# Half-chunk attention from chunk 8 on, and k and v by head through the weights' buffers, in a fused retention and FFN kernel

## The chip, the core and the metric

The kernel runs on one core of a Trainium2 chip. The metric is the device time of one execution in microseconds (us). The engines are named as in the profile: PE is TensorE's matmul, PEld its weight load, DVE is VectorE, ACT is ScalarE, POOL is GpSimd, SP is SyncE, which here issues every DMA.

## What is computed

A recurrent retention layer (batch 4, 8 heads, 768 tokens, head dimension 64) whose output goes through a feed-forward layer with squared ReLU (512 to 2048 to 512), all inputs and the output in float32:

```
for t in range(S):
    state = gamma * state + outer(k[:, :, t], v[:, :, t])      # per batch and head
    y[:, :, t] = scale * q[:, :, t] @ state
x = y as [3072 tokens, 512]
out = relu(x @ w_in) ** 2 @ w_out
```

## The kernel before, in words

**Chunks.** The 3072 tokens are 24 chunks of 128, six to a batch; chunk m is number i = m mod 6 of its batch. Inside a chunk the recurrence is done as matrix products: scores of k against q, a mask, scores times v, plus q times the state that the chunks before have left (`s_bd`). The factors of gamma are multiplied into q and k (`scale_q`, `scale_kv`, `scale_k2`). Heads go in four pairs; "block-diagonal" buffers (`k_bd`, `v_bd`, `s_bd`, `ks_bdp`) hold one head of the pair on partitions 0 to 63 and the other on 64 to 127, with zeros beside them, so that one 128-row matmul serves both heads.

**Three ways of doing a chunk.** Chunks 0 to 3 are done as two pairs ahead of everything else. Chunks 4 to 11 take whole chunks (`attend`): 8 score matmuls of 128 columns (L421) in two steps with a mask each (L428, DVE), 4 state matmuls of 128 columns (L447) and 4 + 8 output matmuls of 128 columns (L476, L484); the PSUM state `c_ps` then also holds products across the two heads of a pair, which nobody reads. Chunks 12 to 23 take two halves of 64 tokens (`attend2`): 8 score matmuls of 64 columns (L681) with one mask (L688), 2 x 4 state matmuls of 64 columns (L708) into a compact `c_ps`, and 8 + 8 output matmuls of 64 columns (L730, L737). q is transposed by PE up to chunk 7 and by DMA from chunk 8 on; k likewise, and for chunks 8 to 11 DVE spreads the DMA's result into `k_bd` (`spread_k`, L410).

**The FFN** runs in blocks of 4, 2, 2, ... chunks. Its matmuls (L777 for the first product, L835 for the second) fill PE; they are cut into pieces of 0.86 to 0.89 us. Pieces are numbered on from 5: block 0 has 12 of the first product (places 5 to 16) and 16 of the second (17 to 32); block 1 is 33 to 40 and 41 to 48, block 2 is 49 to 56 and 57 to 64, and so on by 16.

**The order is written by hand.** `put(n, step, m)` queues a step of the attention, a load or a cast behind piece n; `before(n)` emits the steps of place n in the order of their `put`, and the squares of h after them. Each engine runs its own instructions strictly in that order, waiting on semaphores; so a step that waits holds all that stands behind it on its engine. That holds for SP too: a DMA that waits for its input or its buffer holds every later load and store.

**Loads.** Weights come into `wstage`, 5 buffers of 1 MB, in the order w_in 0 to 3, w_out 0 to 3, and are cast to bf16. k and v of chunks 4 to 11 come a chunk at a time into `ldpool` (L113); those of chunks 12 to 23 in groups of three chunks, head by head, into `grpool` (L129, 16 DMAs of 96 KB a group). `pack_constants` and the zeros of the half-chunk buffers (`zero_off_diagonal`, L329) are made at places 50 to 64.

Of the kernel before, what the change touches and what calls it, by code (L numbers as in the profile page):

```python
# [9 lines left out]
FP32 = mybir.dt.float32  # L10
# [4 lines left out]
ALU = mybir.AluOpType  # L15
# [4 lines left out]
LDBUFS = 4  # L20

# [12 lines left out]
def kernel(  # L34
# [32 lines left out]
    ldpool = ctx.enter_context(tc.tile_pool(name="ldpool", bufs=LDBUFS // 2))  # L67
    grpool = ctx.enter_context(tc.tile_pool(name="grpool", bufs=2))
    qspool = ctx.enter_context(tc.tile_pool(name="qspool", bufs=2))
    kspool = ctx.enter_context(tc.tile_pool(name="kspool", bufs=4))  # L70
# [6 lines left out]
    wstage = ctx.enter_context(tc.tile_pool(name="wstage", bufs=5))  # L77
# [43 lines left out]
    def group_loads(m):  # L121

        b, i = chunks[m]
        for name, src, to in (("kg", k, raw_k), ("vg", v, raw_v)):
            t = grpool.tile([P, 2 * GROUP, NPAIR, D], FP32, name=name)
            for h in range(H):
                p, hh = divmod(h, 2)
                rows = slice(64 * hh, 64 * (hh + 1))
                nc.sync.dma_start(  # L129
                    t[rows, :, p, :],  # L130
                    src[b, h, i * C : (i + GROUP) * C, :].rearrange("(w s) d -> s w d", s=64),
                )
                yield
            for j in range(GROUP):
                to[m + j] = t[:, 2 * j : 2 * j + 2].rearrange("s u p d -> s (u p) d")

    w_in_v = moe_w_in.rearrange("(cb p) f -> p cb f", p=P)
# [3 lines left out]
    def load_w_in(g, parts=1):  # L141
        t = wstage.tile([P, NCB, FQ], FP32, name="w_stage")
        n = FQ // parts
        for j in range(parts):
            nc.sync.dma_start(
                t[:, :, j * n : (j + 1) * n], w_in_v[:, :, g * FQ + j * n : g * FQ + (j + 1) * n]
            )
        staged["in", g] = t

    def load_w_out(g):  # L150
        t = wstage.tile([P, FPQ, DM], FP32, name="w_stage")
        nc.sync.dma_start(t[:], w_out_v[:, g * FPQ : (g + 1) * FPQ, :])
        staged["out", g] = t
# [16 lines left out]
    halves = [slice(0, 64), slice(64, 128)]  # L170
# [160 lines left out]
    def scale_q(m):  # L331
        b, i = chunks[m]
        qs = qspool.tile([P, 2, H, D], BF16, name="qs")
        nc.vector.tensor_tensor(  # L334
            out=qs[:],
            in0=raw_q.pop(m).rearrange("s h r d -> s r h d"),
            in1=qf[:, i : i + 2, :, None].to_broadcast([P, 2, H, D]),
            op=ALU.mult,
        )
        at[m]["qs"] = qs  # L340

    def scale_kv(m):
        b, i = chunks[m]
        ks = kspool.tile([P, H, D], BF16, name="ks")
        nc.vector.tensor_tensor(
            out=ks[:],
            in0=raw_k.pop(m)[:],
            in1=kf[:, i, :, None].to_broadcast([P, H, D]),
            op=ALU.mult,
        )  # L350
# [47 lines left out]
    def dma_transpose_k(m):  # L398
        a = at[m]
        kT = kTpool.tile([P, 2 * NPAIR, C], BF16, name="kT")  # L400
        nc.sync.dma_start_transpose(kT[:, 0:NPAIR], a["ks"].rearrange("s h d -> s (h d)"))
        a["kT"] = kT

    def spread_k(m):
        a = at[m]
        kT = a.pop("kT")
        k_bd = k_bds[m % 2]
        for hh in range(2):
            rows = slice(64 * hh, 64 * (hh + 1))
            nc.vector.tensor_copy(k_bd[rows, :, hh, :], kT[rows, 0:NPAIR])  # L410
        a["k_bd"] = k_bd

# [24 lines left out]
    def state(m, on_scalar=1):  # L437

        b, i = chunks[m]
        a = at[m]  # L440
        if i == NCH - 1:
            return
        if i == 0:
            c_ps[0] = ps_c.tile([P, NPAIR, 2, D], FP32, name="c_ps")
        c = c_ps[0]
        for p in range(NPAIR):
            nc.tensor.matmul(  # L447
                c[:, p],
                lhsT=a["ks"][:, 2 * p : 2 * p + 2, :],
                rhs=a["v_bd"][:, p, ::3, :],  # L450
                start=(i == 0 and p == 0),
                stop=True,
                skip_group_check=True,
            )
        s_bd = s_bds[m % 2]
        for hh in range(2):
            rows = slice(64 * hh, 64 * (hh + 1))
# [11 lines left out]
    def outputs(m):  # L469
# [4 lines left out]
        for p in range(NPAIR):  # L474
            if i > 0:
                nc.tensor.matmul(  # L476
                    y[:, p, :],
                    lhsT=s_bds[(m - 1) % 2][:, p],
                    rhs=a["qT"][:, :, p, :],
                    start=True,  # L480
                    stop=False,
                )
            for hh in range(2):
                nc.tensor.matmul(  # L484
                    y[:, p, :],
                    lhsT=a["v_bd"][:, p, 2 * hh : 2 * hh + 2, :],
                    rhs=a["pt"][:, p, hh, :],
                    start=(i == 0 and hh == 0),
                    stop=(hh == 1),
                )  # L490
# [12 lines left out]
    def scale_pair_q(m, r, engine=nc.vector):  # L503
        b, i = chunks[m]
        if r == 0:
            at[m]["qs"] = qspool.tile([P, 2, H, D], BF16, name="qs")
        engine.tensor_tensor(
            out=at[m]["qs"][:, r],
            in0=raw_q[m].rearrange("s h r d -> s r h d")[:, r],
            in1=qf[:, i + r, :, None].to_broadcast([P, H, D]),  # L510
            op=ALU.mult,
        )

    def scale_pair_k(m, r):
        b, i = chunks[m]
        at[m]["ks"] = pair_view(ks_bd2s[m // 2])
        nc.vector.tensor_tensor(
            out=at[m]["ks"][:, r],
            in0=raw_k[m][:, r],
            in1=kfp[:, i + r, :, None].to_broadcast([P, H, D]),  # L520
            op=ALU.mult,
        )
# [115 lines left out]
    def scale_k2(m):  # L638
# [232 lines left out]
    scale_pair_q(0, 0)  # L871
    scale_pair_q(0, 1)
# [8 lines left out]
    scale_pair_q(2, 0, nc.gpsimd)  # L881
    scale_pair_q(2, 1, nc.gpsimd)
# [50 lines left out]
    def attend_q(m, scaled, transposed):  # L933
        if m % 2 == 0:
            put(scaled, scale_q, m)
            put(transposed, dma_transpose_q if m >= DMA_FROM else transpose_q, m)

# [15 lines left out]
    def attend2(m, d):  # L953
        attend_q(m, d - 17, d - 15)
        put(d - 15, scale_k2, m)
        put(d - 15, cast_v2, m)
        put(d - 13, transpose_k2, m)
        put(d - 6, state2, m, 0)
# [26 lines left out]
    for m, d in zip(range(8, NCHUNK), done):
        if m < PACK_FROM:
            attend(m, d - 15 if d < 70 else d - 16, (d - 13, d - 7, d - 5, d - 3, d))
        else:
            attend2(m, d)
        if m + 3 < PACK_FROM:  # L990
            put(d - 13, load, m + 3)
        elif m + 3 < NCHUNK and (m + 3) % 2 == 0:
            put(d - 13, load_q, m + 3)
    for m, place in zip(range(PACK_FROM, NCHUNK, GROUP), (43, 67, 92, 116)):
        loads = group_loads(m)
        for j in range(2 * H):
            put(place + 3 * j // 2, next, loads)
        put(place + 3 * H, next, loads, None)
# [43 lines left out]
```

## Time and profile before

| what | us |
|---|---|
| runs shown | 215.21, 242.04, 214.72 (median 215.21) |
| the profiled execution | 214.73 |
| its span, first to last instruction | 212.9 |
| PE busy in the span | 204.5 (96%) |
| DVE, ACT, POOL busy | 129.4, 116.2, 50.6 |
| w_in_bf casts (L291), first start | 15.5 |
| w_out_bf casts by POOL (L301), first start | 29.2 |
| first half-chunk matmul (L708) | 101.5 |

Durations below are of the profiled execution. "Mean ns of one" of a matmul holds the way through the array; what a matmul takes from PE is the distance of its start to the next one's start, which the chain of waits shows as the share of a run of matmuls.

### The profile page before, as it was taken

Reading aid. Unit: us, or ns where it says so; the run is one execution under the profiler, and the core shown is the slowest. Engines: PE = TensorE matmul, PEld = TensorE weight load, DVE = VectorE, ACT = ScalarE, POOL = GpSimd, SP = SyncE. Lnnn points to the kernel's source line nnn. Section 1 sums busy time; section 2 is a strip of 40 time slices with the busy share of each in tenths; the row PEclk is TensorE's granted clock in tenths of the full one; section 3 lists DMA queues with packets and bytes.
Section 4 is the critical chain, followed back from the end, with each engine's and each line's share of the span. In section 5 each row is a group of like instructions: output and inputs, shape, how many; then the busy total and the mean of one; then the engine's idle time right before and its main releaser. Section 6 shows DMA issues by size and latency. Waiting matters only on the chain.

```text
span 212.9 us, 5128 instructions
## 1 busy us (share of the span) xinstructions
PE 204.5 (96%) x2077; PEld 142.1 (67%) x2077; DVE 129.4 (61%) x257; ACT 116.2 (55%) x216; POOL 50.6 (24%) x106
## 2 busy tenths in 40 slices
PE   5789999999999999999999999999999999999994
PEld 1467644558966975875875875875965965965853
DVE  4777875265585696796495595593694693640410
ACT  8365885358853643652663663652753754643631
POOL 5332466221110411025121323008122223000000
PEclk9889999999999999999999999999999999999999
DMA  6999999999969898599698698998795452401102
GB/s 162 290 317 383 386 386 258 293 242 274 276 172 201 199 197 145 161 207 182 164 197 191 154 189 188 152 194 202 164 240 127 99 80 72 102 0 49 52 0 99
DMA packets 90551, 39.65 MB, mean 186 GB/s; under 512 B 66336, under 2 KB 84000, under 8 KB 90528
## 3 DMA queue, kind: packets, MB, share of 16 engines
q1 hardware_dynamic: 90528, 39.33, 79.4%
q8 instruction: 16, 0.26, 0.6%
q14 instruction: 7, 0.06, 0.1%
HBM read 27.26 MB, written 6.29 MB: 158 GB/s over the span
## 4 chain that ended last, share of the span: by engine, by line
PE 90%; ACT 2%; DVE 2%; DMA 2%; POOL 1%; issue 1%; POOLq 0%; ACTq 0%; DVEq 0%
PE psf L835 38%; PE psf L777 38%; DMA qn<-in_q_dram 2%; PE st L421 2%; PE y L484 1%; PE st L681 1%; PE y L737 1%; PE y L730 1%; PE c_ps L708 1%; PE y L313 1%; DVE pt L568 1%; PE c_ps L585 1%; PE psf L544 1%; ACT osb L845 1%; PE c_ps L447 1%
## 5 line engine op out<-in xcount | busy, mean ns | idle before, releaser
L777 PE MATMUL psf<-xt,w_in_bf 128*128 128x256 bf16 (+2 forms) x880 | 90.7, 259 | 0.2 <-ACT xt L492 0.2
L835 PE MATMUL psf<-w_out_bf,h 128*128 128x512 bf16 (+2 forms) x400 | 89.6, 371 | 0.0
L777 PEld LDWEIGHTS <-w_in_bf 128*128 128x128 bf16 x880 | 71.3, 98 | 11.8 <-issue 0.3
L786 ACT ACTIVATE h<-psf 128x512 bf16<-128x512 f32 x96 | 57.0, 597 | 22.2 <-PE psf L777 19.6
L835 PEld LDWEIGHTS <-h 128*128 128x128 bf16 x400 | 36.3, 98 | 35.1
L757 DVE TENSOR_TENSOR h<-h 128x512 bf16<-128x512 bf16 x96 | 43.1, 467 | 21.0 <-ACT h L786 20.2
L845 ACT ACTIVATE osb<-psf 128x512 f32<-128x512 f32 (+2 forms) x25 | 14.5, 580 | 28.6 <-PE psf L835 28.6
L718 DVE CAST s_bd<-c_ps 64x256 bf16<-64x256 f32 x22 | 9.4, 427 | 27.4 <-ACT s_bd L717 27.1
L656 POOL CAST v<-vg 128x512 bf16<-128x512 f32 x12 | 8.1, 674 | 56.3 <-PE c_ps L708 21.0
L659 POOL CAST v_bd<-vg 64x512 bf16<-64x512 f32 x24 | 16.4, 682 | 15.0 <-PE y L737 14.1
L428 DVE TENSOR_TENSOR pt<-st,cmask 128x512 bf16<-128x512 f32 x16 | 11.1, 692 | 12.5 <-PE st L421 12.3
L643 DVE TENSOR_TENSOR ks_bdp<-kg,kf 64x512 bf16<-64x512 f32 x24 | 18.3, 762 | 0.4
L353 POOL CAST v_bd<-vn 128x512 bf16<-128x512 f32 x8 | 5.7, 718 | 36.2 <-PE y L484 29.1
L744 ACT ACTIVATE xt<-y 128x512 bf16<-128x512 f32 x12 | 8.9, 742 | 9.6 <-PE y L737 9.6
L334 DVE TENSOR_TENSOR qs<-qn,qf 128x1024 bf16<-128x1024 f32 x10 | 12.1, 1213 | 2.1 <-DMA qn<-in_q_dram 2.0
L717 ACT ACTIVATE s_bd<-c_ps 64x256 bf16<-64x256 f32 x22 | 8.1, 367 | 8.8 <-PE c_ps L708 8.8
L301 POOL CAST w_out_bf<-w_stage 128x512 bf16<-128x512 f32 x12 | 7.8, 689 | 5.5 <-DMA w_stage<-in_moe_w_out_dram 5.5
L492 ACT ACTIVATE xt<-y 128x512 bf16<-128x512 f32 x8 | 6.0, 749 | 5.5 <-PE y L484 5.2
L688 DVE TENSOR_TENSOR pt<-st,cmask 128x512 bf16<-128x512 f32 x12 | 8.3, 691 | 0.4
L313 PE MATMUL y<-ident 128*128 128x512 bf16 (+1 forms) x13 | 5.8, 558 | 2.1 <-POOL ident L199 2.1
L708 PEld LDWEIGHTS <-ks_bdp 128*128 128x128 bf16 x88 | 5.6, 98 | 2.6
L737 PE MATMUL y<-pt,v_bd 128*128 128x64 bf16 x96 | 7.0, 193 | 0.0
(99 smaller groups left out, 167.1 us busy)
## 6 DMA issues: line engine op xcount, KB each, us to landing
qn<-in_q_dram SPq DMA_DIRECT2D x12, 512.0 KB, 4.9
out_dram<-osb SPq DMA_DIRECT2D x23, 256.0 KB, 2.5
w_stage<-in_moe_w_out_dram SPq DMA_DIRECT2D x4, 1024.0 KB, 12.2
w_stage<-in_moe_w_in_dram SPq DMA_DIRECT2D x3, 1024.0 KB, 11.8
kg<-in_k_dram SPq DMA_DIRECT2D x32, 96.0 KB, 3.6
vg<-in_v_dram SPq DMA_DIRECT2D x32, 96.0 KB, 3.4
kn<-in_k_dram SPq DMA_DIRECT2D x8, 256.0 KB, 5.6
vn<-in_v_dram SPq DMA_DIRECT2D x8, 256.0 KB, 5.6
```

Source lines behind the costliest of these rows:

```text
L334: nc.vector.tensor_tensor(out=qs[:], in0=raw_q.pop(m).rearrange("s h r d -> s r h d"), in1=qf[:, i : i + 2, :, None].to_broadcast([P, 2, H ...
L428: nc.vector.tensor_tensor(out=a["pt"][:, 2 * half : 2 * half + 2], in0=st[:], in1=cmask.rearrange("s r t -> s (r t)")[:, None, None, :].to ...
L643: nc.vector.tensor_tensor(out=ks[rows, :, hh, :], in0=kn[rows], in1=kf2[rows, i].rearrange("s u p -> s (u p)")[:, :, None].to_broadcast([6 ...
L659: nc.gpsimd.tensor_copy(v_bd[rows, :, hh, :], vn[rows])
L718: nc.vector.tensor_copy(s_bd[halves[1], :, 1, :], c[halves[1]])
L737: nc.tensor.matmul(yv, lhsT=a["v_bd"][:, u * NPAIR + p], rhs=a["pt"][:, u * NPAIR + p, :].rearrange("s (r t) -> s r t", r=2), start=not inter,
L744: nc.scalar.activation(xts[tb][:, :, off : off + C].rearrange("e p (s r) -> e p r s", r=2), y[:], AF.Copy,)
L757: nc.vector.tensor_mul(hv, hv, hv)
L777: nc.tensor.matmul(hp, lhsT=w_in_bf[g][:, cb, fq * 128 : (fq + 1) * 128], rhs=xts[tb][:, cb, cols], start=(cb == 0), stop=(cb == NCB - 1),)
L786: nc.scalar.activation(hv, hp[:], AF.Relu)
L835: nc.tensor.matmul(op[:], lhsT=h_of(tb, f)[:, 0, j * C : (j + 1) * C], rhs=w_out_bf[g][:, fq, cols], start=(f == 0), stop=(f == NFB - 1),)
L845: nc.scalar.activation(osb[:, cols], op[:], AF.Copy)
```

## The change

`PACK_FROM` goes from 12 to 8: chunks 8 to 11 are done by `attend2` too. So the state that chunks 6 and 7 leave (batch 1) is kept in the compact form that `state2` goes on with: head by head, 8 matmuls with 64 columns of weights and 64 of v, where there were 4 of 128 by 128. `s_bd` is taken in turn from three buffers everywhere. `dma_transpose_k` and `spread_k` go. `scale_q` becomes two instructions, one for each row parity. One pool of four buffers of 1.5 MB (`stage`) replaces `wstage` and `grpool`: weights use two thirds of a buffer, and later k or v of up to six chunks come into one, by 8 DMAs, one for each head (128 KB for chunks 8 to 11, 192 KB for 12 to 17 and 18 to 23). A chunk's k is then [u, pair, d] inside the buffer, with steps. The order of the four w_in and the first w_out loads at the start is as it was. `pack_constants` moves from place 50 to 28, the ten zeroing memsets from 51 to 64 to 29 to 38.

```diff
-LDBUFS = 4
-DMA_FROM = 8
-PACK_FROM = 12
-GROUP = 3
+PACK_FROM = 8
...
-    grpool = ctx.enter_context(tc.tile_pool(name="grpool", bufs=2))
-    kspool = ctx.enter_context(tc.tile_pool(name="kspool", bufs=4))
+    kspool = ctx.enter_context(tc.tile_pool(name="kspool", bufs=2))
-    wstage = ctx.enter_context(tc.tile_pool(name="wstage", bufs=5))
+    stage = ctx.enter_context(tc.tile_pool(name="stage", bufs=4))
...
+    def stage_tile(size):
+        t = stage.tile([P, 2 * NCH * NPAIR * D], FP32, name="stage")
+        return t[:, 0:size]
+
+    def batch_loads(m, name):
+        b, i = chunks[m]
+        src, to = (k, raw_k) if name == "k" else (v, raw_v)
+        t = stage_tile(2 * NCH * NPAIR * D)
+        t = t.rearrange("s (p w d) -> s p w d", p=NPAIR, d=D)
+        size = NCH - i
+        for j in range(size):
+            to[m + j] = t[:, :, 2 * j : 2 * j + 2].rearrange("s p u d -> s u p d")
+        for hh, rows in enumerate(halves):
+            for p in range(NPAIR):
                 nc.sync.dma_start(
+                    t[rows, p, 0 : 2 * size],
+                    src[b, 2 * p + hh, i * C :].rearrange("(w s) d -> s w d", s=64),
                 )
                 yield
...
+    def scale(engine, out, by, table):
+        engine.tensor_tensor(
+            out=out, in0=by, in1=table[:, :, None].to_broadcast([P, H, D]), op=ALU.mult
         )
+    def scale_q(m, r, engine=nc.vector):
+        b, i = chunks[m]
+        if r == 0:
+            at[m]["qs"] = qspool.tile([P, 2, H, D], BF16, name="qs")
+        scale(engine, at[m]["qs"][:, r], raw_q[m][:, :, r], qf[:, i + r])
...
         if i == 0:
-            c_ps[0] = ps_c.tile([P, NPAIR, 2, D], FP32, name="c_ps")
+            c_ps[0] = ps_c.tile([P, NPAIR, D], FP32, name="c_ps")
...
+        else:
+            for p in range(NPAIR):
+                for hh, head in enumerate(halves):
+                    nc.tensor.matmul(
+                        c[head, p, :],
+                        lhsT=a["ks"][:, 2 * p + hh, :],
+                        rhs=a["v_bd"][:, p, 3 * hh, :],
+                        start=(i == 0 and p == 0),
+                        stop=True,
+                        skip_group_check=True,
+                    )
+        s_bd = s_bds[(2 * m + 1) % 3]
...
+    def attend2(m, d, before, q_at, k_at, turn_at, v_at):
+        if m % 2 == 0:
+            put(q_at, scale_q, m, 0)
+            put(q_at + 1, scale_q, m, 1)
+            put(q_at + 2, dma_transpose_q, m)
+        put(k_at, scale_k2, m)
+        put(v_at, cast_v2, m)
+        put(turn_at, transpose_k2, m)
+        put(max(d - 6, before), state2, m, 0)
         put(d - 5, scores2, m)
         put(d - 3, state2, m, 1)
         put(d, outputs2, m)
...
-    put(50, pack_constants)
+    put(28, pack_constants)
     for j, t in enumerate([s_bds[2]] + ks_bd2s + v_bd2s):
         for hh in range(2):
-            put(51 + 3 * j + hh, zero_off_diagonal, t, hh)
...
-    done = [55, 62, 70] + [78 + 8 * j for j in range(13)]
-    for m, place in ((8, 29), (9, 31), (10, 36)):
-        put(place, load, m)
...
+            put(29 + 2 * j + hh, zero_off_diagonal, t, hh)
+    put(29, load_q, 8)
+    put(41, load_q, 10)
+    done = [57, 62] + [70 + 8 * j for j in range(14)]
+    ahead = {8: (47, 48, 48), 9: (52, 53, 53), 10: (57, 59, 58)}
+    for m, d in zip(range(PACK_FROM, NCHUNK), done):
+        attend2(m, d, done[m - PACK_FROM - 1] if m > PACK_FROM else 0,
+                d - 18, *ahead.get(m, (d - 15, d - 13, d - 15)))
+        if m >= 12 and m % 2 == 0:
+            put(d - 29, load_q, m)
+    places = {
+        (8, "k"): [30 + j for j in range(8)],
+        (8, "v"): [38 + j for j in range(8)],
+        (12, "k"): [52 + j for j in range(8)],
+        (12, "v"): [60 + j for j in range(8)],
+        (18, "k"): [84 + 2 * j for j in range(8)],
+        (18, "v"): [100 + 2 * j for j in range(8)],
+    }
```

More of the change, by code (lines that the diff above doesn't have):

```diff
@@ L66 @@
     ldqpool = ctx.enter_context(tc.tile_pool(name="ldqpool", bufs=2))
-    ldpool = ctx.enter_context(tc.tile_pool(name="ldpool", bufs=LDBUFS // 2))
-    grpool = ctx.enter_context(tc.tile_pool(name="grpool", bufs=2))
+    ldpool = ctx.enter_context(tc.tile_pool(name="ldpool", bufs=2))
     qspool = ctx.enter_context(tc.tile_pool(name="qspool", bufs=2))
-    kspool = ctx.enter_context(tc.tile_pool(name="kspool", bufs=4))
+    kspool = ctx.enter_context(tc.tile_pool(name="kspool", bufs=2))
     qTpool = ctx.enter_context(tc.tile_pool(name="qTpool", bufs=3))
@@ L119, in load @@
         load_kv(m)
-    def group_loads(m):
+    def stage_tile(size):
+        t = stage.tile([P, 2 * NCH * NPAIR * D], FP32, name="stage")
+        return t[:, 0:size]
+    def batch_loads(m, name):
         b, i = chunks[m]
[L124 to L128, printed above, removed]
+        src, to = (k, raw_k) if name == "k" else (v, raw_v)
[6 more added lines that the diff above has]
+            for p in range(NPAIR):
                 nc.sync.dma_start(
-                    t[rows, :, p, :],
-                    src[b, h, i * C : (i + GROUP) * C, :].rearrange("(w s) d -> s w d", s=64),
+                    t[rows, p, 0 : 2 * size],
+                    src[b, 2 * p + hh, i * C :].rearrange("(w s) d -> s w d", s=64),
                 )
                 yield
-            for j in range(GROUP):
-                to[m + j] = t[:, 2 * j : 2 * j + 2].rearrange("s u p d -> s (u p) d")
+    halves = [slice(0, 64), slice(64, 128)]
     w_in_v = moe_w_in.rearrange("(cb p) f -> p cb f", p=P)
@@ L141, in load_w_in @@
     def load_w_in(g, parts=1):
-        t = wstage.tile([P, NCB, FQ], FP32, name="w_stage")
+        t = stage_tile(NCB * FQ).rearrange("s (c f) -> s c f", c=NCB)
         n = FQ // parts
@@ L150, in load_w_out @@
     def load_w_out(g):
-        t = wstage.tile([P, FPQ, DM], FP32, name="w_stage")
+        t = stage_tile(FPQ * DM).rearrange("s (f n) -> s f n", f=FPQ)
         nc.sync.dma_start(t[:], w_out_v[:, g * FPQ : (g + 1) * FPQ, :])
@@ L169 @@
         nc.gpsimd.memset(lng[:, h : h + 1], float(np.log(gammas[h])))
-    halves = [slice(0, 64), slice(64, 128)]
     def exponents(pattern, step, name, logs, parts=(slice(0, P),)):
@@ L329, in zero_off_diagonal @@
         nc.vector.memset(t[halves[hh], :, 1 - hh, :], 0.0)
-    def scale_q(m):
-        b, i = chunks[m]
[L333 to L340, printed above, removed]
+    def scale(engine, out, by, table):
[3 more added lines that the diff above has]
+    def scale_q(m, r, engine=nc.vector):
+        b, i = chunks[m]
+        if r == 0:
+            at[m]["qs"] = qspool.tile([P, 2, H, D], BF16, name="qs")
+        scale(engine, at[m]["qs"][:, r], raw_q[m][:, :, r], qf[:, i + r])
     def scale_kv(m):
@@ L344, in scale_kv @@
         ks = kspool.tile([P, H, D], BF16, name="ks")
[L345 to L350, printed above, removed]
+        scale(nc.vector, ks, raw_k.pop(m), kf[:, i])
         v_bd = v_bds[m % 2]
@@ L396, in dma_transpose_q @@
         give_qT(m, qT)
[L398 to L411, printed above, removed]
     def scores(m, half, pool=ps_st, name="st"):
@@ L443, in state @@
         if i == 0:
-            c_ps[0] = ps_c.tile([P, NPAIR, 2, D], FP32, name="c_ps")
+            c_ps[0] = ps_c.tile([P, NPAIR, D], FP32, name="c_ps")
         c = c_ps[0]
[L446 to L457, printed above, removed]
+        if b == 0:
+            for p in range(NPAIR):
+                nc.tensor.matmul(
+                    c[:, p],
+                    lhsT=a["ks"][:, 2 * p : 2 * p + 2, :],
+                    rhs=a["v_bd"][:, p, ::3, :],
+                    start=False,
+                    stop=True,
+                    skip_group_check=True,
+                )
+        else:
+            for p in range(NPAIR):
+                for hh, head in enumerate(halves):
+                    nc.tensor.matmul(
+                        c[head, p, :],
+                        lhsT=a["ks"][:, 2 * p + hh, :],
+                        rhs=a["v_bd"][:, p, 3 * hh, :],
+                        start=(i == 0 and p == 0),
+                        stop=True,
+                        skip_group_check=True,
+                    )
+        s_bd = s_bds[(2 * m + 1) % 3]
+        for hh, head in enumerate(halves):
+            of = c[head, :, hh, :] if b == 0 else c[head]
             if hh < on_scalar:
-                nc.scalar.activation(s_bd[rows, :, hh, :], c[rows, :, hh, :], AF.Copy)
+                nc.scalar.activation(s_bd[head, :, hh, :], of, AF.Copy)
             else:
-                nc.vector.tensor_copy(s_bd[rows, :, hh, :], c[rows, :, hh, :])
+                nc.vector.tensor_copy(s_bd[head, :, hh, :], of)
     def xt_of(m):
@@ L477, in outputs @@
                     y[:, p, :],
-                    lhsT=s_bds[(m - 1) % 2][:, p],
+                    lhsT=s_bds[(2 * m - 1) % 3][:, p],
                     rhs=a["qT"][:, :, p, :],
@@ L501, in pair_view @@
         return t.rearrange("s c hh d -> s (c hh d)").rearrange("s (r h d) -> s r h d", r=2, h=H)
[L503 to L512, printed above, removed]
     def scale_pair_k(m, r):
@@ L516, in scale_pair_k @@
         at[m]["ks"] = pair_view(ks_bd2s[m // 2])
[L517 to L522, printed above, removed]
+        scale(nc.vector, at[m]["ks"][:, r], raw_k[m][:, r], kfp[:, i + r])
     def cast_pair_v(m, on_scalar=False):
@@ L643, in scale_k2 @@
             nc.vector.tensor_tensor(
-                out=ks[rows, :, hh, :],
+                out=ks[rows, :, hh, :].rearrange("s (u p) d -> s u p d", u=2),
                 in0=kn[rows],
-                in1=kf2[rows, i].rearrange("s u p -> s (u p)")[:, :, None].to_broadcast(
-                    [64, 2 * NPAIR, D]
-                ),
+                in1=kf2[rows, i, :, :, None].to_broadcast([64, 2, NPAIR, D]),
                 op=ALU.mult,
@@ L655, in cast_v2 @@
         v2 = v2pool.tile([P, 2 * NPAIR, D], BF16, name="v2")
-        nc.gpsimd.tensor_copy(v2[:], vn[:])
+        nc.gpsimd.tensor_copy(v2.rearrange("s (u p) d -> s u p d", u=2), vn)
         v_bd = v_bd2s[m % 2]
         for hh, rows in enumerate(halves):
-            nc.gpsimd.tensor_copy(v_bd[rows, :, hh, :], vn[rows])
+            nc.gpsimd.tensor_copy(
+                v_bd[rows, :, hh, :].rearrange("s (u p) d -> s u p d", u=2), vn[rows]
+            )
         at[m].update(v2=v2, v_bd=v_bd)
@@ L870 @@
     keep_awake(6, pool=ps_y, name="y")
-    scale_pair_q(0, 0)
-    scale_pair_q(0, 1)
+    scale_q(0, 0)
+    scale_q(0, 1)
     transpose_pair(0, "q", 0, *tp)
@@ L880 @@
     transpose_pair(0, "k", 1, *f, on_scalar=False)
-    scale_pair_q(2, 0, nc.gpsimd)
-    scale_pair_q(2, 1, nc.gpsimd)
+    scale_q(2, 0, nc.gpsimd)
+    scale_q(2, 1, nc.gpsimd)
     scores_pair(0, 0, (st, f))
@@ L931, in put @@
         parts.setdefault(place, []).append((what, args))
[L933 to L936, printed above, removed]
     for m in range(PAIRED):
@@ L941, in attend @@
     def attend(m, scaled, places):
-        by_dma = m >= DMA_FROM
-        attend_q(m, scaled, scaled if by_dma else places[0])
+        if m % 2 == 0:
+            put(scaled, scale_q, m, 0)
+            put(scaled, scale_q, m, 1)
+            put(places[0], transpose_q, m)
         put(places[0], scale_kv, m)
-        if by_dma:
-            put(places[0], dma_transpose_k, m)
-        put(places[1], spread_k if by_dma else transpose_k, m)
+        put(places[1], transpose_k, m)
         put(places[2], scores, m, 0)
@@ L951, in attend @@
         put(places[4], outputs, m)
[L953 to L958, printed above, removed]
+    def attend2(m, d, before, q_at, k_at, turn_at, v_at):
+        if m % 2 == 0:
+            put(q_at, scale_q, m, 0)
[5 more added lines that the diff above has]
+        put(max(d - 6, before), state2, m, 0)
         put(d - 5, scores2, m)
@@ L975 @@
     attend(7, None, (40, 42, 44, 46, 49))
-    put(50, pack_constants)
+    put(28, pack_constants)
     for j, t in enumerate([s_bds[2]] + ks_bd2s + v_bd2s):
         for hh in range(2):
-            put(51 + 3 * j + hh, zero_off_diagonal, t, hh)
-    done = [55, 62, 70] + [78 + 8 * j for j in range(13)]
-    for m, place in ((8, 29), (9, 31), (10, 36)):
-        put(place, load, m)
[L985 to L998, printed above, removed]
+            put(29 + 2 * j + hh, zero_off_diagonal, t, hh)
[16 more added lines that the diff above has]
+    }
+    for (m, name), at_places in places.items():
+        loads = batch_loads(m, name)
+        for place in at_places:
+            put(place, next, loads)
     def before(n):
```

## The prediction, made before the changed kernel was run

> **What bounds the kernel now.** I read the page's busy shares and its slices first.
>
> ```profile
> PE 204.5 (96%) x2077; PEld 142.1 (67%) x2077; DVE 129.4 (61%) x257; ACT 116.2 (55%) x216; POOL 50.6 (24%) x106
> ...
> PEclk9889999999999999999999999999999999999999
> DMA  6999999999969898599698698998795452401102
> ```
>
> PE is full, at full clock from the fourth slice on, and DMA is near its limit up to about 145 us. As a busy share can hide waits, I then took the starts of all matmuls: from 21 us on, the distance from one start to the next exceeds the array's own time by more than 0.03 us only three times, by 0.35, 0.05 and 0.43 us. So there are two prizes: PE work, and these 0.8 us. What a matmul costs PE stands in the chain of waits (start, us, what):
>
> ```profile
> 14.36 0.55 PE c_ps L585 x8
> ...
> 45.74 0.22 PE c_ps L447 x4
> ...
> 61.13 0.45 PE y L484 x8
> ...
> 101.93 0.12 PE c_ps L708 x4
> ...
> 102.92 0.23 PE st L681 x8
> ```
>
> 128 columns cost 55.7 ns, 64 columns 29 ns, each with weights of its own. The two stalls are in the timeline (start, us, engine, what):
>
> ```profile
> 49.07 0.74 ACT L492 ACTIVATE xt<-y 128x512 bf16<-128x512 f32 x1
> ...
> 49.86 1.05 PE L777 MATMUL psf<-xt,w_in_bf 128*128 128x128 bf16 x16 [0.19 <-ACT xt L492]
> ...
> 71.19 0.22 DVE L177 CAST ex_k_f<-ex_k_i 128x48 f32<-128x48 int32 x1 [1.51 <-POOL ex_k_i L175]
> ...
> 72.43 0.38 PE L421 MATMUL st<-qT,k_bd 128*128 128x128 bf16 x4 [0.27 <-DVE pt L428]
> ```
>
> At 49.5 block 1 waits for `xt` behind a full ACT; at 72 pack_constants made DVE wait for POOL, the mask behind it came late, and PE waited 0.43 us. Last the DMA transposes of k and SP's own timeline:
>
> ```profile
> L665 SPq DMA_TRANSPOSE kT<-ks_bdp x12: 1239/1292/2412, 95.2 to 181.5; - x12
> ...
> DMA to landing us min/median/max: 3.1/3.4/4.6
> ```
>
> ```profile
> 62.45 1.75 SPq L393 DMA_TRANSPOSE qT<-qs  x1
> 64.29 1.21 SPq L401 DMA_TRANSPOSE kT<-ks  x1
> 65.55 0.57 SPq L113 DMA_DIRECT2D kn<-in_k_dram  x1
> ```
>
> A half-chunk kT takes 3.1 to 4.6 us from issue to landing; qT(8) leaves only at 62.45, when `scale_q` is through (1.22 us from 60.45). Every landing in this trace comes in the order of issue.
>
> **Part by part.** The sum is made against the profiled execution, 214.73 us: its span of 212.9 and 1.83 around it; it is 0.48 below the median of the runs shown.
>
> *PE work of chunks 8 to 11.* Removed: 24 matmuls of 55.7 ns a chunk (20 in chunk 11, which leaves no state): 3 x 1.337 + 1.114 = 5.12 us. Added: 32 of 29 ns (28 in chunk 11): 3 x 0.928 + 0.812 = 3.60. PE being full, all of it counts: -1.52. A rule of the Trainium skill speaks against this: "TensorE: Matmul & The Clock Gate", section Back-to-back issue gap, says that weight load and matmul together set the spacing in a real kernel, about 81 ns at 128 columns; if the spacing then hardly fell with the columns, the part would come out above zero. Rows L447 and L708, 56 and 29 ns with their own weights, do not agree, and I keep them.
>
> *State of chunks 6 and 7.* 8 x 55.7 = 0.45 out, 16 matmuls with 64 columns of weights in. No row has that shape: the nearest in columns is L708, 16 x 29 = 0.46; above it L585 (half the rows of the array), 69 ns, 1.10; below, two halves side by side, 0.23. I take L708, +0.02, bounds -0.2 and +0.65.
>
> *pack_constants, 50 to 28.* The 0.43 us at 72 go. At place 28 (44.0 us) POOL starts it behind the `v_bd` cast that ends at 44.55; L353's end to the last iota took 1.0 us at 70.16, so DVE has its input at 45.55 and the table's exponential, in ACT's queue ahead of the first `osb` copy, ends at 46.3. That copy began at 45.56: ACT is 0.74 late, has 0.43 idle before the next, and some 0.4 are left when it comes to the `xt` that PE already waits for at 49.5. So +0.4 (bounds 0 and 0.75). The ten memsets (0.17 to 0.27, 2.5 us) go into DVE's idle time of 46 to 58; uncovered, masks would be 0.3 late at most. Net 0.
>
> *Four buffers instead of five at the start.* The first w_out load must now wait until w_in 0 is cast, 19.1 instead of 14.3 us; SP then is one cast behind: w_out 1 at 22.85, w_out 2 at 26.0 (before 22.85), and q, k, v of chunk 4 stand behind these. But w_in 3 lands at 26.45 and then a megabyte every 2.7 us: w_out 0 lands at 29.15 and w_out 2 at 34.6 either way, if they are queued some 3 us before their turn at 26.4 and 31.9. They are: 0. If that cover went, the first w_out cast at 29.2, and PE's second product at 33.4, would shift by what the queue ran dry.
>
> *Chunk 8, the start of the new chain.* The queue: (8,k) follows q8 at 48 us and lands by 59. Of (8,v), three go, then qT(8) at place 41 holds SP until DVE has scaled q, 62.3; five DMAs of 0.6 and the store of chunk 4 are behind it, so the last v is issued at 67.3 and lands at 70.2 (2.9; vg rows 2.5 to 5.9). POOL's first cast (0.67) ends at 70.9, when PE comes to state2(8,0) at place 51: 70.9. Nothing, or up to 1. `scale_k2(8)` follows DVE's `s_bd` copy (66.5 + 0.43), 2 x 0.72: 68.4; kT(8) goes behind the store of chunk 5 at 68.95 and lands 3.3 later, 72.3. PE is at scores2(8) (place 52) at 71.9: +0.4 (bounds 0 and 1.5). The new steps in [u, pair, d] may cost DVE up to L643's longest, 1.1 for 0.69; that is inside.
>
> *Chunk 9.* From the mask of chunk 8 (72.6 + 0.7) DVE does `scale_k2(9)`, 1.45: 74.75; kT(9) lands 3.1 to 3.4 later, 78.0. PE has four pieces of 0.89, one of 0.865 and 0.7 of attention up to scores2(9): 72.55 + 5.13 = 77.7. +0.3 (0 to 1.5).
>
> *Chunk 10.* SP: kT(9) 74.8, one k load, qT(10) when both halves of q are scaled (76.7), three loads of 192 KB, q12, two more, then kT(10), 81.8. Landings in order: qT(10) 80.4; a kg of 96 KB takes 0.40 where they follow each other, so 5 x 0.8; q12 1.85 (as q4 after w_out 2: 34.63 to 36.51); kT itself 1.0: 87.2. PE reaches scores2(10) at place 65: 78.25 + 7 x 0.865 + 0.7 + 0.875 = 85.9. +1.3 (0 to 2.5). The Trainium skill, "DMA: Bandwidth & Descriptors", section Queues, rings and completion order, says that completion on such a queue is not in the order of issue; by it kT(10) might land early and the sum be 1.3 less. The landings of this trace are all in order, so I keep the wait.
>
> *The rest.* kT(11) lands at 94.5 by the same sum, PE wants it at 95.2; from chunk 12 on the distance from transpose to scores is 8 places, as before. `scale_q` in two (2 x 0.69 for 1.22), two `s_bd` copies for one, against `spread_k` (2 x 0.29) and a second mask (0.69) gone: DVE is 61% busy and nobody waits. DMA bytes are the same.
>
> Sum: -1.52 + 0.02 - 0.43 + 0.4 + 0.4 + 0.3 + 1.3 = +0.47: 215.2 us.
>
> **The rivals.**
>
> *The waits do not come.* For it: all three waits hang on sums of several queue times, each within 1.3 us; a shorter issue of qT(8) (1.23 for 1.75) pulls chunk 8 through. Against: 8 places between transpose and scores have become 4, 4 and 6. 214.73 - 1.52 - 0.43 + 0.02 = 212.8, with the 0.4 at ACT 213.2.
>
> *Slower: the k transposes of chunks 8 to 10 arrive late each time.* One queue carries the batch loads and the transposes; if a kT takes 5.5 us, as qT does behind queued loads (5.7 at 92.67), the three waits are 2.6, 2.5 and 3.0: 8.1 for my 2.0, 214.73 - 1.5 + 8.1 = 221.3. It turns the result from about 1.9 us of wait a chunk on. A second cost then follows, which the granted clock shows by windows (us, PE busy and matmuls, then PEld, DVE, ACT, POOL, clock):
>
> ```profile
> 5.23:8.64 3.41, 1.86 (x18) 1.01 (x18) 2.43 (x4) 1.79 (x3) 0.00 (x0) 1.00 1.22 290
> 8.65:12.06 3.41, 3.37 (x43) 2.07 (x44) 3.04 (x6) 1.15 (x2) 2.04 (x2) 0.50 1.22 290
> 12.06:15.47 3.41, 3.10 (x65) 2.19 (x63) 2.02 (x5) 2.30 (x5) 1.17 (x2) 1.00 1.14 323
> ```
>
> After 3.41 us in which PE was busy 55%, the clock is halved for 3.41 us; 91% kept it. A wait of 1.5 us or more in one window may thus cost 1.7 more.
>
> *Every matmul costs the same.* If 64 columns cost the 55.7 ns of 128, chunks 8 to 11 gain 8 x 4 x 0.0557 = +1.8 instead of -1.5: 218.5. Rows L681, L708 and L737 speak against it.
>
> *The earlier loads do not happen.* If w_out 0 misses its turn (queue dry at 26.4) or a buffer wait holds SP, PE stalls in the second product of block 0 by 2 to 5 us: 217 to 220.
>
> **How the numbers follow.** Forecast, waits in part: 0.50, 214 to 217. No waits: 0.30. Late transposes: 0.11. Equal spacing: 0.03. Dry queue: 0.06. The likeliest is 215.2; the range reaches down to the case without waits, 212.6, and up to the forecast's upper bounds together with part of the late cases, 218.8. Two per cent is 4.3 us, about what a measurement of this kernel can tell from no change. No case reaches 210.4 (0.02 for what I overlook); beyond 219.5 lie most of the late transposes and the end of the dry queue (0.11); the rest, 0.87, is within.
>
> **What would show it.** Right: L681 x128 at 29 ns a start, no L410, no pack_constants at 70 us; PE gaps at place 52, 57 and 65 ended by DMA kT; first w_out cast still at 29.2. Wrong: no such gaps; or gaps above 1.9 us, half-clock slices behind 70 us, a w_out cast after 30.

## The result, and the profile after

The changed kernel takes 222.73 us (median of 4 runs, 222.19 to 223.05) where the kernel before takes 214.97: 1.0365 times, 95% interval 1.0332 to 1.0398. (The kernel before has four runs; the one of 242.04 us is a slow one, counted in its median and left out of the ratio.) It is slower, and outside the range. The profiled execution took 223.05 us, its span is 221.3, 8.4 more than before. Line numbers shift: L755 and L813 are now the FFN's products, L659 the half-chunk scores, L686 the half-chunk state, L643 and L389 the transposes of k and q, L132 the batch loads.

The page's busy shares, granted clock and DMA slices answer to the first lines shown above:

```profile
PE 204.4 (92%) x2095; PEld 141.5 (64%) x2117; DVE 130.6 (59%) x263; ACT 117.3 (53%) x220; POOL 56.5 (26%) x114
...
PEclk9999999999999999889999999999999999999999
DMA  6999999999899299999958999999537423701102
```

PE is as long at work as before but 92% of the span instead of 96%: the loss is waiting. The DMA slices (5.5 us each) show a hole, the 2 at 72 to 77 us, and the clock drops from 89 to 100. The page's chain of waits by engine is 63% PE and 21% DMA; before it was 90% PE and 2% DMA. In order of time (start, us, what):

```profile
67.53 3.77 DMA stage<-in_v_dram
71.31 0.05 issue
71.36 0.91 POOL v L632
...
76.54 3.12 DMA kT<-ks_bdp
...
86.49 6.11 DMA kT<-ks_bdp
...
96.20 7.10 DMA kT<-ks_bdp
```

The end is now set by v of chunk 8 and the k transposes of chunks 9, 10 and 11. The last two take 6.1 and 7.1 us from issue to landing; 4.6 was the longest before. What SP did between them (start, us, engine, what):

```profile
70.79 0.62 SPq L132 DMA_DIRECT2D stage<-in_k_dram  x1
76.54 1.25 SPq L643 DMA_TRANSPOSE kT<-ks_bdp  x1
77.83 0.60 SPq L132 DMA_DIRECT2D stage<-in_k_dram  x1
78.97 1.25 SPq L389 DMA_TRANSPOSE qT<-qs  x1
80.27 2.80 SPq L132 DMA_DIRECT2D stage<-in_k_dram  x3
83.12 0.66 SPq L89 DMA_DIRECT2D qn<-in_q_dram  x1
83.83 2.55 SPq L132 DMA_DIRECT2D stage<-in_k_dram  x2
86.49 3.07 SPq L643 DMA_TRANSPOSE kT<-ks_bdp  x1
```

From 71.4 SP stands behind kT(9), which DVE releases at 76.5. Behind it are one k load, qT(10), five more k loads with q of chunk 12 among them, and then kT(10); an eighth k load follows. Windows (us, then PE, PEld, DVE, ACT, POOL busy, granted clock, DMA share, GB/s; packets of one engine overlap, so the share can pass 1) show both halves of it. First the kernel before, then the changed one:

```profile
74.80:79.70 4.90, 4.90 (x60) 3.58 (x58) 4.68 (x12) 2.55 (x4) 0.96 (x1) 1.00 1.08 211
79.70:104.50 24.80, 24.80 (x216) 17.51 (x215) 17.36 (x35) 11.35 (x20) 4.88 (x7) 1.00 0.90 171
```

```profile
74.80:79.70 4.90, 4.17 (x72) 3.52 (x70) 4.77 (x9) 3.30 (x7) 2.90 (x5) 1.00 0.35 70
79.70:104.50 24.80, 18.57 (x171) 12.58 (x174) 13.81 (x28) 8.84 (x17) 2.94 (x4) 0.93 1.31 192
```

And what it did to the clock:

```profile
85.37:88.78 3.41, 2.36 (x19) 1.30 (x17) 0.55 (x2) 1.88 (x4) 1.20 (x2) 1.00 1.27 226
88.78:92.19 3.41, 0.00 (x0) 0.00 (x0) 0.00 (x0) 0.00 (x0) 0.00 (x0) 1.00 1.35 193
92.19:95.61 3.42, 2.96 (x21) 2.22 (x22) 1.02 (x2) 0.60 (x1) 0.00 (x0) 0.50 1.27 226
```

For 4.9 us DMA runs at a third of the share that it had in the kernel before; for the 25 us after, it is fuller, 1.31 for 0.90. PE stands for a whole window of 3.41 us, and the next one has half the clock.

The longest wait stands in PE's timeline:

```profile
92.65 0.61 PE L659 MATMUL st<-qT,kT 128*128 128x64 bf16 x8 [4.91 <-DMA kT<-ks_bdp]
```

From the starts of the matmuls, as in the prediction, the loss adds up (us that PE lost, or gained, against the kernel before):

| where | measured | in the sum of the prediction |
|---|---|---|
| `xt` at 49 (0.91 for 0.35) | +0.56 | +0.4 |
| state2(8,0), for v of chunk 8 | +0.89 | 0 |
| scores2(8), for kT(8) | 0 | +0.4 |
| state2(9,0), for DVE's copy of `s_bd` | +0.75 | 0 |
| scores2(9), for kT(9) | +0.26 | +0.3 |
| scores2(10), for kT(10) | +5.08 | +1.3 |
| half clock from 92.65 to 95.61 | +1.48 | 0 |
| scores2(11), for kT(11) | +1.37 | 0 |
| pack_constants at 72, gone | -0.43 | -0.43 |
| PE work of chunks 6 to 11, by the starts | -1.27 | -1.50 |
| first 33 us (-0.39), k of chunk 7 (L376, +0.16) | -0.23 | 0 |
| sum | +8.46 | +0.47 |

The span grew by 8.4. The starts bear out the -1.52 of chunks 8 to 11; the state of chunks 6 and 7 (L441) cost 0.25 us where +0.02 was taken. From the last score matmul to the next one of the FFN it is 0.41 us there, and was 0.28. What made the first 33 us shorter stays open.

### The profile page after: what moved, and what is told of

Its sections match the earlier page's. It is cut to its first block, busy times and chain, and to the rows that moved or that the text cites. A ratio compares the mean times of both kernels' runs of the same rounds, so it can differ in the third digit from the quotient of the medians.

```text
span 221.3 us, 5174 instructions
## 1 busy us (share of the span) xinstructions
PE 204.4 (92%) x2095; PEld 141.5 (64%) x2117; DVE 130.6 (59%) x263; ACT 117.3 (53%) x220; POOL 56.5 (26%) x114
## 4 chain that ended last, share of the span: by engine, by line
PE 63%; DMA 21%; SPq 5%; DVE 4%; ACT 2%; POOL 2%; issue 1%; ACTq 0%
PE psf L813 29%; PE psf L755 26%; DMA kT<-ks_bdp 7%; DMA stage<-in_moe_w_in_dram 5%; DMA stage<-in_moe_w_out_dram 4%; DMA vn<-in_v_dram 3%; SPq L97 3%; PE st L659 2%; DMA stage<-in_v_dram 2%; PE y L715 1%; PE y L708 1%; PE c_ps L686 1%; DVE h L735 1%; SPq L147 1%; DVE w_in_bf L294 1%
## 5 line engine op out<-in xcount | busy, mean ns | idle before, releaser
L755 PE MATMUL psf<-xt,w_in_bf 128*128 128x256 bf16 (+2 forms) x879 | 91.9, 261 | 0.8 <-ACT xt L486 0.7
L813 PE MATMUL psf<-w_out_bf,h 128*128 128x512 bf16 (+2 forms) x379 | 87.3, 370 | 1.2 <-issue 0.2
L755 PEld LDWEIGHTS <-w_in_bf 128*128 128x128 bf16 x880 | 71.8, 99 | 12.8 <-issue 0.9
L813 PEld LDWEIGHTS <-h 128*128 128x128 bf16 x400 | 36.1, 98 | 35.3
L696 DVE CAST s_bd<-c_ps 64x256 bf16<-64x256 f32 x29 | 12.4, 428 | 33.8 <-ACT s_bd L695 33.2
L632 POOL CAST v<-stage 128x512 bf16<-128x512 f32 x16 | 11.3, 709 | 75.7 <-PE c_ps L686 29.4
L635 POOL CAST v_bd<-stage 64x512 bf16<-64x512 f32 x32 | 21.6, 674 | 24.9 <-PE y L715 23.9
L621 DVE TENSOR_TENSOR ks_bdp<-stage,kf 64x512 bf16<-64x512 f32 x32 | 24.1, 754 | 0.6
L722 ACT ACTIVATE xt<-y 128x512 bf16<-128x512 f32 x16 | 11.9, 743 | 13.5 <-PE y L715 13.5
L333 DVE TENSOR_TENSOR qs<-qn,qf 128x512 bf16<-128x512 f32 x22 | 15.1, 696 | 3.4 <-DMA qn<-in_q_dram 3.4
L695 ACT ACTIVATE s_bd<-c_ps 64x256 bf16<-64x256 f32 x29 | 10.7, 368 | 11.3 <-PE c_ps L686 9.2
L659 PE MATMUL st<-qT,kT 128*128 128x64 bf16 x128 | 6.6, 196 | 6.2 <-DMA kT<-ks_bdp 6.1
L659 PEld LDWEIGHTS <-kT 128*128 128x128 bf16 x128 | 5.8, 100 | 8.7 <-DMA kT<-ks_bdp 7.1
L686 PEld LDWEIGHTS <-ks_bdp 128*128 128x128 bf16 x116 | 7.2, 98 | 4.7 <-issue 0.8
L686 PE MATMUL c_ps<-v,ks_bdp 128*128 128x64 bf16 x116 | 8.1, 193 | 1.3 <-POOL v L632 0.7
L708 PE MATMUL y<-qT,s_bd 128*128 128x64 bf16 x120 | 9.1, 193 | 0.0
```

The costliest lines, as they stand in the source:

```text
L333: engine.tensor_tensor(out=out, in0=by, in1=table[:, :, None].to_broadcast([P, H, D]), op=ALU.mult)
L621: nc.vector.tensor_tensor(out=ks[rows, :, hh, :].rearrange("s (u p) d -> s u p d", u=2), in0=kn[rows], in1=kf2[rows, i, :, :, None].to_bro ...
L635: nc.gpsimd.tensor_copy(v_bd[rows, :, hh, :].rearrange("s (u p) d -> s u p d", u=2), vn[rows])
L659: nc.tensor.matmul(st[:, c, :], lhsT=kT[:, c, :], rhs=half_of(a["qT"], p, u), start=True, stop=True,)
L686: nc.tensor.matmul(c[:, p, :], lhsT=a["ks"][:, u * NPAIR + p], rhs=a["v2"][:, u * NPAIR + p, :], start=(i == 0 and u == 0 and p == 0), sto ...
L696: nc.vector.tensor_copy(s_bd[halves[1], :, 1, :], c[halves[1]])
```

## The experiments

Theory 1, formed on these lines: kT(10) is late because it stands in one queue behind q12 and five 192 KB loads, which kT(9) and qT(10) had held back. The first four runs were made together, beside 214.09 for the kernel before. All five are single runs, and runs of the kernel before beside the later experiments lie between 214.06 and 215.53. So differences of under about 1 us among these times say nothing; the waits in the traces do.

**Other order of the loads.**

```diff
-            put(d - 29, load_q, m)
+            put(49 if m == 12 else d - 29, load_q, m)
-        (12, "k"): [52 + j for j in range(8)],
-        (12, "v"): [60 + j for j in range(8)],
+        (12, "k"): [50, 51, 52, 59, 60, 61, 62, 63],
+        (12, "v"): [66, 67, 68, 69, 70, 70, 70, 70],
```

> The changed kernel with the same loads in another order: q of chunk 12 and three of the eight k loads of chunks 12 to 17 go ahead of kT(9), where DMA ran dry from 74.8 to 79.7 us, the other five behind kT(10), and the v loads behind kT(11). Theory 1 (kT(10) was late because it stood behind q12 and five 192 KB loads that kT(9) and qT(10) had held back on SP): the wait of 5.1 us at the scores of chunk 10 falls below 0.5, the half-clock window of 3.4 us behind it goes, chunk 11 waits at most 1.5: 215 to 217.5 us. Rival 2 (the half-chunk steps of chunks 9 and 10 stand too close to their scores, so that DVE delivers k too late whatever the queue holds): over 2 us of wait stay at chunk 10, 219 to 221 us.

222.11 us. The wait at chunk 10 was gone, as theory 1 had it and against rival 2; kT(9) now stood behind q12 and three loads and made PE wait 1.76 us; and 4.5 us of wait had moved to chunk 12, whose state wanted v:

```profile
PE c_ps L686 <- POOL v L632: 4.4, 1, 4.4
...
PE st L659 <- DMA kT<-ks_bdp: 1.8, 2, 1.6
```

(The waits of PE: who for whom, us in all, times, longest.) So the place of the wait was explained, and its size was not: theory 1's time was missed by 4.6 us.

**Other layout of the batch buffer.**

```diff
-        t = t.rearrange("s (p w d) -> s p w d", p=NPAIR, d=D)
+        t = t.rearrange("s (w p d) -> s p w d", p=NPAIR, d=D)
```

> The changed kernel with the batch buffer laid out window by window, then pair, as the groups of before had it, so that a load writes 256 bytes at a step of 1 KB into a partition instead of one run of 3 KB; places and sizes as in the changed kernel. A 192 KB load there takes 1.1 to 1.4 us in the order of landing, where 96 KB took 0.40 before. Rival 3 (the new layout makes the loads slower): 0.8 to 0.9 us a load, the wait at chunk 10 falls by about 2 us, 220 to 221 us. Theory 1 with the size alone: 1.1 to 1.4 us as before, wait about 5 us, 222 to 223.5 us.

222.33 us, wait at chunk 10 4.75. The three k loads behind qT(10) still landed 1.03 to 1.25 us apart; the two behind q12 came 0.66 and 0.72 apart, but q12 itself took 2.63 instead of 1.81. From the landing of qT(10) to that of kT(10) it was 8.2 us, and 8.8 in the changed kernel. Rival 3 wanted a wait shorter by about 2 us and falls; the layout is worth 0.6 us there at most.

**k steps of chunks 9 and 10 earlier.**

```diff
-    ahead = {8: (47, 48, 48), 9: (52, 53, 53), 10: (57, 59, 58)}
+    ahead = {8: (47, 48, 48), 9: (48, 50, 53), 10: (55, 56, 58)}
```

> The changed kernel with the k steps of chunk 9 at places 48 and 50 (were 52 and 53) and of chunk 10 at 55 and 56 (were 57 and 59); the loads stay where they are. kT(9) then leaves SP right behind kT(8), and kT(10) stands behind three k loads and no longer behind q12 and two more. Theory 1: no wait at chunks 9 and 10, but kT(11) still stands behind q12 and the loads that were not moved, and the wait moves to chunk 11, 2 to 4 us: 217 to 220 us. Rival 2: no wait at 9, 10 or 11, 214 to 216 us.

221.86 us. No wait for kT(9) or kT(10) was left; kT(8) landed 1.05 late, and 4.9 us stood at chunk 11. The move was as theory 1 said; the wait was over its 2 to 4 us, and the time 2 us over its range.

**v of chunk 8 first, pack_constants at 43.**

```diff
-    put(28, pack_constants)
+    put(43, pack_constants)
-        (8, "v"): [38 + j for j in range(8)],
+        (8, "v"): [36, 37, 38, 38, 39, 39, 40, 40],
```

> The changed kernel with all eight v loads of chunk 8 ahead of q's transpose of chunk 8, and pack_constants at place 43 instead of 28. PE's gap at 49 us falls from 0.91 to about 0.35, that of the first half-chunk state (0.89 at 71 us) to 0.2 or less. Theory 1: the wait at chunk 10 stays at 4.5 to 5.5 us, so the time is 222 to 222.8 us. If the early gaps were what pushes the rest back (a rival in which the chain of chunk 8 sets the wait at chunk 10), the wait falls by more than 1 us, 219.5 to 221.5 us.

221.24 us: the time lies in the rival's range and 0.8 under theory 1's, too little to tell them apart with single runs. The wait at chunk 10 does: it was 5.16, as theory 1 had it (4.5 to 5.5), and did not fall as the rival wanted. The gap at 49 us fell to 0.36 and the wait for v of chunk 8 went, but kT(8) then came 0.68 late. Early gains are mostly waited away later: in these four runs about 5 us stand wherever the queue is longest. That called for a theory of the amount.

**Theory 5: too much is due too soon.** A batch load brings a head's k or v for six chunks, and chunk 12 can't start before the last of its 16 loads has landed. Before, a group was three chunks. So by place 71 1.5 MB more are due. In this run the same buffer is filled in two halves of three chunks (`lo` is 0 or 3), the second half later. All steps, and the loads for chunks 8 to 14, stand where the change had put them; the loads from chunk 15 on get new places:

```diff
-                    t[rows, p, 0 : 2 * size],
-                    src[b, 2 * p + hh, i * C :].rearrange("(w s) d -> s w d", s=64),
+                    t[rows, p, 2 * lo : 2 * (lo + size)],
+                    src[b, 2 * p + hh, i * C : (i + size) * C].rearrange(
+                        "(w s) d -> s w d", s=64
+                    ),
...
         (12, "k"): [52 + j for j in range(8)],
         (12, "v"): [60 + j for j in range(8)],
-        (18, "k"): [84 + 2 * j for j in range(8)],
-        (18, "v"): [100 + 2 * j for j in range(8)],
+        (15, "k"): [70 + 2 * j for j in range(8)],
+        (15, "v"): [86 + j for j in range(8)],
+        (18, "k"): [95 + j for j in range(8)],
+        (18, "v"): [103 + j for j in range(8)],
+        (21, "k"): [111 + 2 * j for j in range(8)],
+        (21, "v"): [126 + 2 * j for j in range(8)],
```

> The changed kernel with each batch of six chunks loaded in two halves of three (96 KB a load, into the same buffer): at places 52 to 67 only k and v of chunks 12 to 14 are loaded, those of 15 to 17 at 70 to 93; the steps of chunks 8 to 11 stand where they stood. Theory 5 (moved loads only moved the wait, because a batch of six chunks must be complete before chunk 12 can start, so 1.5 MB more than before crowd the queue from 77 to 105 us): kT(10) comes some 3 us earlier, the wait at chunk 10 is 1.5 to 2.5 us, no wait at chunk 11, a half-clock window at most: 216.5 to 219 us. Rival 6 (the held queue alone: SP stands behind kT(9) and qT(10), whatever the size of the loads): the wait at chunk 10 stays over 4 us, 220 to 222 us. Under theory 1's sizes a 96 KB load lands 0.55 to 0.65 us behind the one before it.

217.25 us. The wait at chunk 10 was 1.80, chunk 11 had none, no window after the first 12 us had half the clock: inside theory 5's ranges, outside rival 6's. SP still stood behind kT(9) up to 76.0, but kT(10) left at 84.1 and landed at 88.9:

```profile
81.76 0.89 SPq L89 DMA_DIRECT2D qn<-in_q_dram  x1
82.70 1.30 SPq L139 DMA_DIRECT2D stage<-in_k_dram  x2
84.11 2.26 SPq L652 DMA_TRANSPOSE kT<-ks_bdp  x1
```

One expectation failed: the loads behind qT(10) and q12 landed 0.21 to 0.48 us apart, not 0.55 to 0.65. But the way from the landing of kT(9) to that of kT(10), with the same six loads, qT(10) and q12 between them, was 9.65 us, and 12.94 in the changed kernel: 3.3 us less for six times 96 KB less, 0.55 us for each.

**Steps early, with half and with whole batches.** Both have the k steps as early as the two `ks_bdp` buffers allow, and k of chunk 12 and on in the hole behind kT(9); they differ only in the batches.

```diff
-    put(28, pack_constants)
+    put(43, pack_constants)
-    put(41, load_q, 10)
+    put(42, load_q, 10)
-    ahead = {8: (47, 48, 48), 9: (52, 53, 53), 10: (57, 59, 58)}
+    ahead = {8: (45, 46, 48), 9: (47, 48, 53), 10: (55, 56, 58), 11: (60, 61, 63)}
-        (8, "v"): [38 + j for j in range(8)],
-        (12, "k"): [52 + j for j in range(8)],
-        (12, "v"): [60 + j for j in range(8)],
+        (8, "v"): [36, 37, 38, 38, 39, 39, 40, 40],
+        (12, "k"): [49, 49, 50, 50, 51, 51, 52, 52],
+        (12, "v"): [58, 58, 59, 59, 62, 62, 63, 63],
```

> The half batches and, besides, the k steps as early as their two buffers allow (chunk 8 at places 45 and 46, 9 at 47 and 48, 10 at 55 and 56, 11 at 60 and 61), v of chunk 8 ahead of qT(8), q of chunk 10 behind it, pack_constants at 43, and k of chunks 12 to 14 at 49 to 52, right behind kT(9), where DMA ran dry. If both the held queue and the batches made the loss, no wait over 0.5 us is left from 21 us on and the saved PE work shows: 1.5 to 2.5 us less than the kernel before on the same chip, ratio 0.988 to 0.993. If PE's half-chunk work itself is dearer than its matmul starts say, the ratio is 1.0 or above without waits.

> As the run with all steps early, but with the whole batches of six chunks (192 KB a load) at the same places. Rival 6 (the held queue alone): waits of 0 to 1 us in all, within 1 us of the kernel with half batches. Theory 5: 1.5 MB more stand ahead of the transposes of chunks 10 to 12 and 2 to 5 us of wait are left, at chunk 10, 11 or 12.

With half batches (the other halves at 64 to 72 and 74 to 88, those of chunks 18 to 23 as in the run before) 214.32 us, ratio to the kernel before 0.9981, interval 0.9968 to 0.9994: no wait for a DMA from 21 us on, but one of 0.91 for DVE, where none over 0.5 was expected. The gain was 0.4 us, about a quarter of what was expected or less. With whole batches 219.65 us, with waits of 1.2 at chunk 10 and 2.7 at chunk 11 and a half-clock window behind:

```profile
PE st L659 <- DMA kT<-ks_bdp: 3.6, 2, 2.5
```

Together with the changed kernel these make a square:

| us | whole batches of six | halves of three |
|---|---|---|
| steps where the change put them | 222.73 | 217.25 |
| steps early | 219.65 | 214.32 |

The batch costs 5.5 or 5.3 us, the places 3.1 or 2.9; each stands by itself. (Three of the four corners were run beside 214.7 for the kernel before, the changed kernel beside 214.97, and the two mixed corners are single runs.)

**Two loads of 96 KB for each of 192.** The same bytes at the same places, in twice the DMAs.

```diff
         (12, "k"): [52 + j for j in range(8)],
+        (15, "k"): [52 + j for j in range(8)],
         (12, "v"): [60 + j for j in range(8)],
+        (15, "v"): [60 + j for j in range(8)],
```

(with the loads in halves as above, and likewise for 18 and 21)

> The changed kernel with each 192 KB load issued as two of 96 KB right behind each other at the same place: the same bytes due at the same places, only the size of a DMA differs. If the bytes that are due make the loss (theory 5), the wait at chunk 10 stays at 4.3 to 5.5 us: 221.5 to 223.5 us. If it is the size of one DMA (a rival: 192 KB land 1.05 to 1.3 us apart, two of 96 KB in 0.9), kT(10) comes some 1.5 us earlier, the wait is 3 to 3.7 us: 219.5 to 221 us.

225.9 us, wait at chunk 10 6.5: over both ranges. The size of a DMA is not the cure, but theory 5's number failed too, for a reason that it lacked: SP.

```profile
80.78 5.00 SPq L139 DMA_DIRECT2D stage<-in_k_dram  x6
85.82 0.62 SPq L89 DMA_DIRECT2D qn<-in_q_dram  x1
86.50 2.64 SPq L139 DMA_DIRECT2D stage<-in_k_dram  x4
89.25 1.77 SPq L652 DMA_TRANSPOSE kT<-ks_bdp  x1
```

Back to back, a load costs SP 0.62 us to issue and starts 0.67 behind the one before it; ten of them and q12 hold kT(10) for 8.5 us. The loads themselves were not slower: ten of 96 KB landed in 5.5 us, five of 192 KB in 6.2. But q12 was issued 2.7 us later than in the changed kernel and landed at 91.0 instead of 89.2, and kT(10) at 93.9 instead of 92.6.

**The last wait.** With half batches and early steps, state2(9,1) waited 0.91 us for DVE's copy of `s_bd`, behind `scale_k2(10)` and two squares of h.

```diff
-                d - 18, *ahead.get(m, (d - 15, d - 13, d - 15)))
+                50 if m == 10 else d - 18, *ahead.get(m, (d - 15, d - 13, d - 15)))
```

> The kernel with all steps early and half batches, and q of chunk 10 scaled at places 50 and 51 (was 52 and 53), where DVE idled. There the one wait left was 0.91 us at 79 us: state2(9,1) waited for DVE's copy of s_bd(9,0), which stood behind scale_k2(10). Moving q's two multiplications (1.8 us) ahead brings that copy forward by about 1 us: the wait falls below 0.3, 0.6 to 0.9 us less than that kernel, ratio to the kernel before 0.994 to 0.996. If DVE is as late as before, the wait stays and the ratio is 0.998.

213.55 us, ratio 0.994, interval 0.9925 to 0.9955; the wait fell to 0.31. This version beats both kernels: 1.2 us less than before, where half-chunk work alone was worth 1.5.

## Why the prediction was wrong, by its steps

**Right.** The PE work: L659 and L686 start 29 ns apart where PE does not wait, and the last version, nearly without waits, shows the gain; so the rival of equal spacing is out. The state of chunks 6 and 7 came out dearer, 0.25 us for 0.02, inside its bounds. The 81 ns at 128 columns of the Trainium skill ("TensorE: Matmul & The Clock Gate", section Back-to-back issue gap) are not seen: 56 ns in these traces. pack_constants cost 0.56 at 49 us for 0.4 and gave back 0.43. The first w_out landed at 29.23 (29.15 forecast): four buffers cost nothing at the start.

**Wrong: the term of chunk 10, "+1.3 (0 to 2.5)".** It was 5.08. The forecast had kT(10) land at 87.2 and PE come at 85.9; it landed at 92.6, and PE came at 87.6. Of the 5.4 us that kT(10) was late,

- 3.4 came from the start of the crowd: qT(10) landed at 83.8 instead of 80.4. 2.3 of them are its issue, at 79.0 instead of 76.7: chunk 8's scores came 1.0 late, for v, and their mask another 0.3, behind a square of h; `scale_k2(9)` took 1.95 instead of 1.45, with POOL's casts beside it; and 0.5 passed from the end of `scale_q` to the issue. The other 1.1 are its way to landing, 4.8 us instead of 3.7, behind a k load that alone landed 3.1 us after kT(9), where the forecast had 2.4 for that load and qT(10) together.
- 2.2 came from the size of a load. I had taken 0.40 us for 96 KB from kg loads that landed behind a q load. These had been issued 0.67 us apart and landed 0.40 to 0.48 apart, so they had piled up behind the q load, and that distance is not the time of a load. The five loads of 192 KB took 1.05 to 1.38 us, 1.24 in the mean, not 0.8; the run with halves makes it 0.55 for 96 KB.

The other -0.2 is the transpose itself, 0.8 for 1.0, and q12.

**Missing: the half clock, and chunk 11.** The half clock follows from that wait and was left to a rival. For kT(11) 94.5 was forecast, 103.3 came, and PE wanted it at 102.0. Of these 8.8 us 5.4 came with kT(10). The rest lies between the two transposes, 10.7 us for 7.3: six loads at 1.16 in the mean for 0.8, and kT(11) 2.5 behind the load ahead of it.

**Smaller terms.** At chunk 8 PE waited at the state (0.89, inside "up to 1") and not at the scores (0 for 0.4): the last v landed 3.8 us after its issue, for 2.9, and POOL's cast took 0.90 for 0.67; with PE that late, kT(8) was in time. Of DVE the forecast said that nobody waits: state2(9,0) waited 0.75 us for its copy of `s_bd`.

**Missing: the amount.** "DMA bytes are the same" is nearly true of the whole (39.9 MB on the queue for 39.3) and was taken as the end of the matter. Of what is due before chunk 12 it is wrong: six chunks of k and v instead of three. The square above shows that this one oversight was worth 5.3 to 5.5 us, more than all waits in the forecast together.

**The rival that came nearest**, late transposes on one queue, had the mechanism and nearly the time (221.3 before its half-clock cost), and was given 0.11. Its time is in part luck: it has 8.1 us of wait for kT(8), kT(9) and kT(10), where 5.3 came, nearly all for kT(10). The range stopped at 218.8, short of it.

## What to carry over

Price a load by what is due before its first reader can start, not by bytes in all: a batch that covers six users makes the first one wait for the bytes of all. On a queue in strict order, look for the step that waits for an engine (here a transpose of what DVE makes), count what is issued behind it, and give the hole that it leaves in DMA to loads that are due anyway. And take a transfer's time from a stretch in which like follows like, never from the landings behind a larger one.

## What was not expected of the hardware

**The clock falls after a window that is not idle.** In the changed kernel the window ahead of the half clock was wholly idle. With whole batches and early steps it was not, and the clock was halved all the same (windows, as above):

```profile
95.46:98.87 3.41, 0.88 (x12) 0.45 (x11) 1.15 (x4) 0.17 (x1) 0.00 (x0) 1.00 0.92 134
98.87:102.28 3.41, 3.41 (x10) 1.21 (x8) 1.80 (x3) 0.00 (x0) 0.00 (x0) 0.50 1.38 160
```

The page "TensorE: Matmul & The Clock Gate" of the Trainium skill, section What's actually happening, gives half clock after at least one idle window of about 3.4 us; here 26% busy was too little. How much is enough does not follow from these traces. Each change of the clock in a trace lies a whole number of windows of 3.41 us from the next one. In such windows 55% busy lost the full clock at the start of the kernel before, but 52% kept it in the run with half batches and late steps (1.78 us of 86.85 to 90.26, with most of the wait of 1.80), and 47% in the run with the other order of the loads (1.60 us of 76.81 to 80.22, with most of the wait of 1.76). So the forecast's price, 1.7 us more for a wait of 1.5 us or more in one window, was not due for these two: they cost only themselves.

**DVE beside POOL.** A half `scale_k2` takes 0.67 to 0.69 us alone and mostly 0.93 to 1.1 with a POOL cast beside it for 0.45 us or more, in the kernel before as in the changed one.

**Left open.** What sets the time of a load where the queue is full is not settled. In the run in pairs, eight v loads of 96 KB in a row landed 0.55 to 0.64 us apart while SP started one every 0.67, so that 1.2 us for 192 KB is about the time of two of 96 KB. A stretch of 96 KB loads with SP out of the way was not tried.
